# Attention with a later landing time and an earlier last step of the feature map in its scheduler

## The chip, the cores and the metric

The kernel runs on one core of one Trainium2 chip. The metric is the device time of one execution in microseconds (us). A core has five engines that run their own instruction lists in order: PE (matrix products), DVE (VectorE), ACT (ScalarE), POOL (GpSimd) and SP (SyncE), which here only issues transfers between HBM and the on-chip memory. An engine that waits for something holds up all that stands behind it in its list.

## The reference

Three stages run one after the other: attention, a mixture of experts, and a dense block of two layers. Only the first is touched by the change, and only its scores and its feature map matter here.

```python
B, H, S, D = (4, 8, 576, 64)
scores = scale * np.matmul(q, k.transpose(0, 1, 3, 2))
scores = np.where(causal, -1000000000.0, scores)
scores = scores - scores.max(-1, keepdims=True)
a = np.exp(scores)
a /= a.sum(-1, keepdims=True) + 1e-09
local = np.matmul(a, v)

def phi(x):
    return np.where(x > 0, x, np.exp(x) - 1.0) + 1.0
q_p = phi(q)
mem_ret = np.einsum('bhsd,bhde->bhse', q_p, M_prev)
mem_norm = np.einsum('bhsd,bhd->bhs', q_p, z_prev)[..., None] + 1e-06
mem_out = mem_ret / mem_norm
return (g * mem_out + (1 - g) * local).astype(np.float32)
```

The output of attention goes through `_moe_ref` (gate, one of eight experts per token) and `_moe2_ref` (two dense products), whose code the change leaves alone.

## The kernel before

**Tiles.** Attention works on eight groups, n = 0 to 7: batch n // 2, and heads 0 to 3 or 4 to 7 of it. The 576 rows of a group are cut into three row blocks, x = 0, 1, 2: rows 0 to 255, 256 to 511, 512 to 575. For each row block q and k are loaded into `qn` and `kn` (tile a in the profile), v into one of two tiles `vn`. Groups share the one `qn` and the one `kn`; so a row block of the next group's q can only be loaded when the present group has read it for the last time.

**What is done with q.** For each row block the ACT copies q into an array of rounded values (L594), POOL makes the rest (L599), and the feature map is made in three steps: `exp` on ACT (L629) into `ph`, `relu` on ACT (L631) in place in `qn`, and the last step on DVE (L634), which reads both. That last step is also the last reader of the row block of `qn`. It releases the next group's q load of the same block. k is copied by DVE (L592).

**What a slot is.** Each group has eight slots (four heads, two halves of the rows). In a slot PE makes the scores (L728), DVE takes the row maxima from them (L735, L747, L752), PE turns the maxima with q (L759), ACT evicts that (L764), PE makes the scores once more with the maxima in them (L779, L781, L786, L790), ACT takes `exp` of them (L795, tile pT), and PE multiplies with v (L817, L820). Between the slots stand the transposes of the next group's k and q (PE L644, L647; evicted by ACT L665, L666, L672).

**What else runs there.** 32 pieces of the weights of the third stage are converted beside attention: a load of 512 KB (L321), two ACT steps (L326, L329), two DVE steps (L332, L335), a POOL step (L338) and a store of 256 KB (L341).

**What sets the order.** Every step is a task of `Sched`: an engine, a duration, the tasks it depends on, and a key. `Sched.order` plays the tasks through in a model of time. A free engine takes, of its ready tasks, the one with the lowest key; a task that ends makes its users ready after a latency, `LAT` of its engine (2,300 ns for SP) or its own `lat`. The sequence that comes out is the order in which the instructions of PE, ACT, DVE and POOL are written. SP's transfers are put in place by the tool that builds the program, from the same sequence. On the chip nothing of the model's time is left, only the order. The keys of the feature map are `G[n] - L * f`, with f = `PE1`, `PE2`, `PE3` for its three steps; G[n] is the group's start in the model and L = 4 * (1320.114 + 3696.75) = 20,067 ns. The keys of group 0 are made in another way: `T0 + 5000 + 1000 * x - 1000 * f`.

Of the kernel before, what the change touches and what calls it, by code (L numbers as in the profile page):

```python
# [25 lines left out]
PVB = 2  # L26
LDT = (1310, 1310, 650)
X0, XH, PH0, FIN, RT1, RT2, RW = 86.4, 9571.6, -315.2, -443.3, 4930.3, 5386.7, 1.74
PKH, PKL, PQH, PQL, PE1, PE2, PE3 = 0.19, 1.07, 0.92, 0.72, 0.38, 0.26, -0.09
EK, WS = 39944.504, 485.0  # L30
PT0, PTX, PTH, PT2 = 0.3, -0.1, -0.17, -1427.4
MAN = {ET.PE, ET.Activation, ET.DVE, ET.Pool}
# [2 lines left out]
SP = [[[(0, 0, 0, 128), (1, 128, 0, 256)]], [[(2, 0, 0, 384)], [(3, 0, 0, 512)], [(4, 0, 0, 256)], [(4, 0, 256, 320)]]]  # L35
# [28 lines left out]
class Sched:  # L64
# [5 lines left out]
    def add(self, eng, dur, fn, deps=(), key=0.0, take=(), give=(), lat=None):  # L70
        self.tasks.append((eng, dur, fn, set(d for d in deps if d is not None), key, take, give, lat))
        return len(self.tasks) - 1
# [59 lines left out]
class K:  # L132
# [401 lines left out]
    def group(self, n, b, g, get, put):  # L534
        nc, add, st = self.nc, self.sc.add, self.st
        L, G = 4 * (TA + TB), self.G
        par, h0 = n % 2, G4 * g
        kn, qn, ph, kx, qa = self.kn, self.qn, self.ph, self.kx, self.qa
        qb, vn = self.qb[par], self.vn[par]
# [9 lines left out]
        def load(dst, src, i0, i1):  # L549
            def f():  # L550
                if i1 - i0 == 2:
                    for i in range(i0, i1):
                        nc.sync.dma_start(dst[:, i, :, 0:D], src[b, h0:h0 + G4, rng(i), :].rearrange("h p d -> p h d"))
                else:
                    nc.sync.dma_start(dst[:64, 4, :, 0:D], src[b, h0:h0 + G4, 512:576, :].rearrange("h p d -> p h d"))
            return f
        gs = G[n] - (LD * L if n else 1e6)
        for x, (i0, i1) in enumerate(W):
            lk = add("SP", LDT[x], load(kn, self.k, i0, i1), get(("kuse", n - 1, x)), gs if n else gs + 2 * x)
            lq = add("SP", LDT[x], load(qn, self.q, i0, i1), get(("quse", n - 1, x)), gs + 1 if n else gs + 2 * x + 1)  # L560
            put(("lk", n, x), lk)
            put(("lq", n, x), lq)
            if n == 0:
                self.first |= {lk, lq}
        for x, (i0, i1) in enumerate(W):
            lv = add("SP", LDT[x], load(vn, self.v, i0, i1), get(("vuse", n - 2)) + (get("set") if n == 1 else []), gs + 2 if n else gs + 6 + x)
            put(("lv", n), lv)
            if n == 0:
                self.first.add(lv)
# [703 lines left out]
    def put(self, o, xg, ix, w3, after):  # L1273
        v = [self.axpy(o, xg, ix[:, 1:2].bitcast(F32)), self.axpy(o, xg, w3, slice(64, 128))]
        info = mybir.DependencyInfo(mybir.DependencyClass.NoSync, mybir.DependencyReason.DATA)
        for i in v:
            self.tc.add_manual_dep(i.ins, after.name, info, reason="issue order")
# [423 lines left out]
```

## Time and profile before

| | |
|---|---|
| median of 3 runs | 873.3 us (871.55 to 881.11) |
| profiled execution | 869.84 us, of which its span is 868.2 us |
| attention | about 0 to 300 us of the span |
| experts | about 300 to 470 us |
| dense block | 470 us to the end |

Times in the rows below are us from the start of the span. A row of the timeline reads: start, duration, engine, line, operation, tile written from tiles read, form, number of like instructions merged into the row; in brackets the idle time of the engine ahead of it and who ended that. A row of the stretches reads: stretch and its length, then busy time and number of instructions of PE, PEld (weight loads), DVE, ACT and POOL, then the granted clock of TensorE as a share of full speed, the busy share of the DMA engines, and GB/s.

### The profile page before, as it was taken

To read this page: it belongs to the slowest core of one execution; us is meant where nothing else is said; L and a number is where in the kernel's file an instruction comes from. 1 tells how busy PE (TensorE), PEld (TensorE's weight loads), DVE (VectorE), ACT (ScalarE), POOL (GpSimd) and SP (SyncE) were. 2 spreads that over 40 slices of the span, in tenths; PEclk is the share of its full clock that TensorE was granted. 3 is DMA by queue.
4 is the path that set the end of the run, shared out by engine and by line. 5 is a ranking of instruction groups with operands and counts; after the bars stand their busy time and mean duration, and the time that the engine had idled before them with its cause. 6 is when DMAs were issued, how large, how long until landed. Compare 5 with 4: busy or idle time off the path is not lost. (4 is left out here: it accounts for less than half of the span.)

```text
span 868.2 us, 19498 instructions
## 1 busy us (share of the span) xinstructions
PE 829.6 (96%) x7368; PEld 739.0 (85%) x7368; DVE 614.3 (71%) x1739; ACT 481.3 (55%) x937; POOL 195.7 (23%) x262
## 2 busy tenths in 40 slices
PE   6999999997999799999989999999999999999997
PEld 5788877886888677667657999999999999999997
DVE  6877987787778983786774599665656565656565
ACT  8898977886865742776654455333333333333332
POOL 6546445644532613322220000000000000000000
PEclk9999999998999999999999999999999999999999
DMA  6857547765356586797744201010101010101000
GB/s 144 220 147 229 151 157 177 204 221 128 102 158 256 191 329 186 283 359 252 258 180 137 80 1 51 1 50 1 49 2 49 2 49 2 49 2 49 1 26 25
DMA packets 103946, 107.61 MB, mean 124 GB/s; under 512 B 69661, under 2 KB 69789, under 8 KB 103828
## 3 DMA queue, kind: packets, MB, share of 16 engines
q1 hardware_dynamic: 101190, 100.90, 37.0%
q0 software_dynamic: 2640, 5.21, 1.9%
q8 instruction: 67, 1.10, 0.5%
q14 instruction: 49, 0.40, 0.2%
HBM read 81.57 MB, written 25.86 MB: 124 GB/s over the span
## 5 line engine op out<-in xcount | busy, mean ns | idle before, releaser
L1616 PE MATMUL g<-sw,ah 128*128 128x256 f32 x448 | 126.0, 281 | 0.0
L1615 PE MATMUL g<-sw,ah 128*128 128x256 f32 x448 | 125.7, 281 | 0.0
L1567 DVE SCALAR_TENSOR_TENSOR ua<-ua 128x512 f32<-128x512 f32 x72 | 49.7, 690 | 80.2 <-ACT ua L1516 80.2
L1516 ACT ACTIVATE ah<-ua 128x384 fp32r<-128x384 f32 (+1 forms) x72 | 38.8, 539 | 110.4 <-PE g L1617 82.6
L1516 ACT ACTIVATE ua<-t 128x512 f32<-128x512 f32 x72 | 43.0, 597 | 101.1 <-PE t L1560 101.1
L735 DVE CUSTOM_DVE_ANT_0 v<-t,v 128x512 f32<-128x512 f32 (+4 forms) x160 | 75.3, 471 | 28.1 <-PE t L728 23.2
L1617 PE MATMUL g<-sw,al 128*128 128x256 f32 x320 | 89.8, 281 | 0.0
L1615 PEld LDWEIGHTS g<-sw,ah 128*128 128x128 f32 x448 | 84.4, 188 | 0.0
L1616 PEld LDWEIGHTS g<-sw,ah 128*128 128x128 f32 x448 | 84.3, 188 | 0.0
L795 ACT ACTIVATE pT<-t 128x384 f32<-128x384 f32 (+2 forms) x128 | 62.5, 503 | 23.9 <-PE t L786 13.1
L1557 PE MATMUL t<-x,v 128*128 128x256 f32 x288 | 71.9, 283 | 0.7 <-ACT x L1436 0.7
L1558 PE MATMUL t<-x,a 128*128 128x256 f32 x288 | 71.0, 280 | 0.5 <-DVE a L1103 0.5
L1558 PE MATMUL t<-x,v 128*128 128x256 f32 x288 | 71.1, 279 | 0.0
L1557 PE MATMUL t<-x,a 128*128 128x256 f32 x288 | 71.0, 280 | 0.0
L820 PE MATMUL pv<-vn,pT 128*64 128x65 f32 x1280 | 61.4, 232 | 0.6 <-issue 0.6
L1617 PEld LDWEIGHTS g<-sw,al 128*128 128x128 f32 x320 | 60.9, 190 | 0.0
L820 PEld LDWEIGHTS pv<-vn,pT 128*64 128x64 f32 x1280 | 46.9, 139 | 15.6 <-issue 11.0
L1557 PEld LDWEIGHTS t<-x,v 128*128 128x128 f32 x288 | 54.3, 188 | 1.2 <-ACT x L1436 0.9
L338 POOL TENSOR_TENSOR cg<-cg,v 128x512 int32<-128x512 int32 x32 | 42.5, 1330 | 56.2 <-issue 29.1
L1558 PEld LDWEIGHTS t<-x,a 128*128 128x128 f32 x288 | 54.1, 188 | 0.7 <-DVE a L1103 0.7
L1558 PEld LDWEIGHTS t<-x,v 128*128 128x128 f32 x288 | 54.1, 188 | 0.3
L1557 PEld LDWEIGHTS t<-x,a 128*128 128x128 f32 x288 | 54.1, 188 | 0.0
(371 smaller groups left out, 2317.8 us busy)
## 6 DMA issues: line engine op xcount, KB each, us to landing
c<-in_moe_w_dram SPq DMA_DIRECT2D x32, 512.0 KB, 6.5
va<-in_moe_w_dram SPq DMA_DIRECT2D x21, 512.0 KB, 7.9
v<-in_moe_w_in_dram SPq DMA_DIRECT2D x16, 512.0 KB, 4.9
v<-in_moe_w_out_dram SPq DMA_DIRECT2D x16, 512.0 KB, 4.6
xe<-x SPq DMA_DIRECT2D x18, 256.0 KB, 3.1
out_dram<-xe SPq DMA_DIRECT2D x18, 256.0 KB, 2.2
a<-in_k_dram SPq DMA_DIRECT2D x32, 128.0 KB, 4.4
a<-in_q_dram SPq DMA_DIRECT2D x32, 128.0 KB, 3.2
```

What stands on the lines that cost most here:

```text
L338: nc.gpsimd.tensor_tensor(u["g"], u["g"], u["s"], op=ALU.add)
L735: nc.vector.tensor_tensor_reduce(out=self.y[:R, 0:w], in0=s[:R, o:o + w], in1=self.mb[:R, max(0, MB[i] + c0):max(0, MB[i] + c0) + w], scal ...
L795: nc.scalar.activation(u["pT"][:, o1:o1 + w], u.pop(("t", p))[:, 0:w], AF.Exp, scale=0.125)
L820: nc.tensor.matmul(t[m:m + 64, o:o + 65], u["pT"][:, c + m:c + m + 64], vn[:, j, h], start=(j == 0), stop=(j == i))
L1516: tt_, cp = V.tensor_tensor, lambda o, i: A.activation(o, i, AF.Copy)
L1557: nc.tensor.matmul(o, wih[k][:, fs], xh[:, k], start=(k == 0), stop=False)
L1558: nc.tensor.matmul(o, wil[k][:, fs], xh[:, k], start=False, stop=False)
L1567: V.scalar_tensor_tensor(u, u, 0.01, u, op0=ALU.mult, op1=ALU.max)
L1615: nc.tensor.matmul(o, ah, wh, start=(p == z == 0), stop=False, skip_group_check=True)
L1616: nc.tensor.matmul(o, ah, wl, start=False, stop=False, skip_group_check=True)
L1617: nc.tensor.matmul(o, al, wh, start=False, stop=(p == 7), skip_group_check=True)
```

## The change

Two numbers of the scheduler's model change. Loads of k, q and v get `lat=3500` in place of SP's 2,300 ns, so in the model their users become ready 1,200 ns later. `PE3` goes from -0.09 to 0.1, so the key of the feature map's last step (DVE L634) falls by 0.19 * L = 3,813 ns in groups 1 to 7, and by 190 ns in group 0. Neither adds or removes an instruction. What comes of it is another order.

```diff
-PKH, PKL, PQH, PQL, PE1, PE2, PE3 = 0.19, 1.07, 0.92, 0.72, 0.38, 0.26, -0.09
+PKH, PKL, PQH, PQL, PE1, PE2, PE3 = 0.19, 1.07, 0.92, 0.72, 0.38, 0.26, 0.1
...
-            lk = add("SP", LDT[x], load(kn, self.k, i0, i1), get(("kuse", n - 1, x)), gs if n else gs + 2 * x)
-            lq = add("SP", LDT[x], load(qn, self.q, i0, i1), get(("quse", n - 1, x)), gs + 1 if n else gs + 2 * x + 1)
+            lk = add("SP", LDT[x], load(kn, self.k, i0, i1), get(("kuse", n - 1, x)), gs if n else gs + 2 * x, lat=3500)
+            lq = add("SP", LDT[x], load(qn, self.q, i0, i1), get(("quse", n - 1, x)), gs + 1 if n else gs + 2 * x + 1, lat=3500)
...
-            lv = add("SP", LDT[x], load(vn, self.v, i0, i1), get(("vuse", n - 2)) + (get("set") if n == 1 else []), gs + 2 if n else gs + 6 + x)
+            lv = add("SP", LDT[x], load(vn, self.v, i0, i1), get(("vuse", n - 2)) + (get("set") if n == 1 else []), gs + 2 if n else gs + 6 + x, lat=3500)
```

The order moves on every engine from group 0 to the start of group 5 and is nearly the same from there on. Three places follow.

DVE in group 5, about 202 us into the span of before. L735 is the row maxima of head 1's slot of rows 256 to 575 (its second row reads out the result), L747 and L752 finish them, L332 and L335 belong to the conversion, and L634 is the last step of the feature map of group 6, row block 2. Before:

```order
L735 ISA v_85,m_98<-t,v_85 64x256
L735 ISA m_98 64x1
L332 SCALAR_TENSOR_TENSOR v_85<-v_85 128x512
L735 ISA v_85,m_98<-t,v_85,m_98 64x320
L735 ISA m_98 64x1
L335 TENSOR_SCALAR cg<-cg 128x512
L747 TENSOR_REDUCE m_98<-m_98 128x3
L752 TENSOR_REDUCE v_84<-m_98 128x3x2
L634 SCALAR_TENSOR_TENSOR a_82<-a_82 128x256
```

After the change DVE has there:

```order
L735 ISA v_85,m_96<-t,v_85 64x256
L735 ISA m_96 64x1
L634 SCALAR_TENSOR_TENSOR a_82<-a_82 128x256
L735 ISA v_85,m_96<-t,v_85,m_96 64x320
L735 ISA m_96 64x1
L332 SCALAR_TENSOR_TENSOR v_85<-v_85 128x512
L747 TENSOR_REDUCE m_96<-m_96 128x3
L752 TENSOR_REDUCE v_84<-m_96 128x3x2
L335 TENSOR_SCALAR cg<-cg 128x512
```

The last step stands ahead of a conversion step and of the last part of the row maxima, where it stood behind both; L335 now stands behind the maxima's end.

SP at the same place, as a piece of the difference: the five loads of v of group 6, then the load of q of group 7, row block 2 (L555 into a), and the conversion's stores (L341) and loads (L321).

```order
 L553 DMA vn_90<-in_v_dram 128x4x64 x4
 L555 DMA vn_90<-in_v_dram 64x4x64
-L341 DMA wout<-cg 128x512
-L321 DMA v_85<-in_moe_w_out_dram 128x1024
-L555 DMA a_82<-in_q_dram 64x4x64
+L555 DMA a_82<-in_q_dram 64x4x64
+L341 DMA wout<-cg 128x512
+L321 DMA v_85<-in_moe_w_out_dram 128x1024
 L341 DMA wout<-cg 128x512
 L321 DMA v_85<-in_moe_w_out_dram 128x1024
```

The load of q stands ahead of one store and one load of the conversion.

ACT in group 3, about 137 to 143 us into the span of before: evictions of slots (L764), `exp` of slots (L795) and the copies of q of group 5 (L594, two to a row block). Before:

```order
L764 ACTIVATE q_2446<-t 66x256
L795 ACTIVATE pT<-t 128x320
L764 ACTIVATE q_2461<-t 66x256
L594 ACTIVATE v_84<-a_82 128x8x64 x2
L795 ACTIVATE pT<-t 128x384 x2
L326 ACTIVATE cg<-v_85 128x512
L329 ACTIVATE v_85<-v_85 128x512
L665 ACTIVATE b_86<-t 128x2x256
```

After the change ACT has there:

```order
L764 ACTIVATE q_2453<-t 66x256
L795 ACTIVATE pT<-t 128x320
L672 ACTIVATE b_86<-t 128x2x256
L795 ACTIVATE pT<-t 128x384
L329 ACTIVATE v_85<-v_85 128x512
L594 ACTIVATE v_84<-a_82 128x8x64
L795 ACTIVATE pT<-t 128x384
L594 ACTIVATE v_84<-a_82 128x8x64
L594 ACTIVATE v_84<-a_82 128x4x64
```

The first of the two `exp` stands ahead of the copies of q, with two other steps, and the second between them.

## Rows read from the trace of the kernel before

**Rows 1.** The page's first line: the span.
```profile
span 868.2 us, 19498 instructions
```

**Rows 2.** Stretches: most of attention, the stretch round 210 us, the experts.
```profile
10.00:200.00 190.00, 182.86 (x2161) 154.85 (x2159) 154.95 (x598) 163.47 (x376) 98.31 (x127) 1.00 0.67 183
200.00:220.00 20.00, 15.03 (x140) 12.77 (x138) 12.91 (x45) 11.20 (x28) 9.04 (x10) 0.83 0.48 116
...
300.00:470.00 170.00, 158.46 (x822) 115.09 (x823) 115.38 (x190) 95.10 (x141) 41.21 (x35) 1.00 0.71 250
```

**Rows 3.** Timeline of PE from 198 to 218 us.
```profile
198.20 0.69 PE L820 MATMUL pv<-vn,pT 128*64 128x65 f32 x16
...
205.38 0.35 PE L759 MATMUL t<-idr,v 128*66 128x128 f32 x3 [0.30 <-DVE v L752]
...
214.25 0.69 PE L728 MATMUL t<-c 128*128 128x384 f32 x1 [3.46 <-ACT pT L795]
...
216.50 1.14 PE L820 MATMUL pv<-vn,pT 128*64 128x65 f32 x16
```

**Rows 4.** Timeline of ACT from 207 to 214 us.
```profile
207.29 0.60 ACT L795 ACTIVATE pT<-t 128x512 f32<-128x512 f32 x1 [0.29 <-PE t L786]
213.41 0.42 ACT L594 ACTIVATE v<-a 128x256 fp32r<-128x256 f32 x1 [5.52 <-DMA a<-in_q_dram]
```

**Rows 5.** Timeline of SP from 201 to 207 us.
```profile
201.72 0.65 SPq L555 DMA_DIRECT2D vn<-in_v_dram  x1
203.63 0.34 SPq L341 DMA_DIRECT2D wout<-cg  x1
204.06 0.38 SPq L321 DMA_DIRECT2D v<-in_moe_w_out_dram  x1
206.75 0.65 SPq L555 DMA_DIRECT2D a<-in_q_dram  x1
```

**Rows 6.** Timeline of DVE and POOL from 202 to 207 us.
```profile
202.29 1.86 DVE L332 SCALAR_TENSOR_TENSOR v<-v 128x512 int32<-128x512 int32 x1
202.31 1.29 POOL L338 TENSOR_TENSOR cg<-cg,v 128x512 int32<-128x512 int32 x1
...
204.55 0.41 DVE L335 TENSOR_SCALAR cg<-cg 128x512 int32<-128x512 int32 x1
...
205.06 0.17 DVE L752 TENSOR_REDUCE v<-m 128x6 fp32r<-128x12 f32 x1
205.11 1.31 POOL L338 TENSOR_TENSOR cg<-cg,v 128x512 int32<-128x512 int32 x1
205.15 1.57 DVE L634 SCALAR_TENSOR_TENSOR a<-a 128x256 f32<-128x256 f32 x1
```

**Rows 7.** Line L634, the last step: durations, and what its engine waited for.
```profile
L634 DVE SCALAR_TENSOR_TENSOR a<-a x24: 364/684/1572, 12.8 to 236.9; 128x512 f32<-128x512 f32 x16, 128x256 f32<-128x256 f32 x8
...
  ACT a L631: 0.3, 1
```

**Rows 8.** Line L555, the loads of row block 2: issue to landing.
```profile
DMA to landing us min/median/max: 2.3/3.1/6.0
```

**Rows 9.** One stretch: the matmuls behind the wait of PE at 214 us.
```profile
214.20:218.90 4.70, 4.64 (x30) 4.09 (x31) 2.31 (x9) 3.71 (x10) 0.00 (x0) 0.50 0.00 1
```

**Rows 10.** Timeline of ACT and PE from 141 to 146 us.
```profile
141.01 1.16 ACT L594 ACTIVATE v<-a 128x512 fp32r<-128x512 f32 x2 [2.31 <-DMA a<-in_q_dram]
142.07 0.85 ACT L795 ACTIVATE pT<-t 128x384 f32<-128x384 f32 x2
142.59 0.38 PE L759 MATMUL t<-idr,v 128*66 128x128 f32 x3 [0.58 <-ACT pT L795]
...
145.07 0.49 PE L728 MATMUL t<-c 128*128 128x512 f32 x1 [0.81 <-ACT b L672]
```

**Rows 11.** Line L631, the relu on ACT ahead of the last step: durations.
```profile
L631 ACT ACTIVATE a<-a x24: 406/618/689, 8.4 to 235.4; 128x512 f32<-128x512 f32 x16, 128x256 f32<-128x256 f32 x8
```

**Rows 12.** Timeline of PE in the experts, its longest wait there.
```profile
387.56 5.17 PE L1150 MATMUL s<-a,xs 128*128 128x512 f32 x21 [1.91 <-ACT b L1099]
```

## The prediction

> **What bounds the kernel now.** I read the stretches first, since the change can only act in attention, the first 300 us. Between 10 and 200 us PE is busy for 182.86 of 190 us [rows 2]: PE sets the pace, and no more than 7.14 us of idle time stand there, in short pieces. The stretch from 200 to 220 us is the exception: PE is busy for 15.03 of 20 us, and the granted clock falls to 0.83 in the mean. So I followed that one hole back, engine by engine, in the timelines.
>
> PE stands still for 3.46 us before 214.25, and waits there for ACT's `exp` [rows 3]. ACT had finished the `exp` before that at 207.89 and then stood still for 5.52 us, until 213.41, because the next instruction in its list, the copy of q of group 7, row block 2, waited for the landing of that q [rows 4]. The load of this q was issued at 206.75, although SP had been done with the v loads ahead of it at 202.37 and with the conversion's transfers at 204.44 [rows 5]. It could not go earlier, because the buffer was still being read: DVE's last step of the feature map of group 6, row block 2, ran from 205.15 to 206.72 [rows 6]. So the chain is: last step late on DVE, load late, ACT's copy late, `exp` behind the copy late, PE idle. It has a second price. Behind the hole the granted clock is 0.50, which is the 1.2 GHz level, for the whole stretch from 214.20 to 218.90, with PE busy for 4.64 us in it [rows 9]. Sixteen like matmuls take 1.14 us there and 0.69 us at 198.20 at the full 2.4 GHz level [rows 3].
>
> **The change part by part.** No instruction is added or removed, so each term is a wait that goes or comes.
>
> *The late load.* On DVE the last step of group 6, row block 2, now stands directly behind the row maxima that ended just ahead of 202.29. Ahead of it go one L332, one L735, one L335 and the end of the maxima, which was over at 205.23 [rows 6]. The step so starts at about 202.3 in place of 205.15. Its duration is bounded by 0.36 us (the shortest of the 24) and 1.57 us (the longest, which is this very one) [rows 7]. It ends between 202.7 and 203.9. SP has nothing ahead of the load but the v loads, over at 202.37, so the load is issued between 202.7 and 203.9, which is 2.9 to 4.1 us earlier. From issue to landing, loads of this size take 2.3 to 6.0 us with a median of 3.1 [rows 8]; in before this one took about 6.6 us (206.75 to the copy's start at 213.41), with a store and a 512 KB load issued shortly ahead of it [rows 4, 5], both of which now stand behind it. With the median the q lands between 205.8 and 207.0, before ACT gets there at 207.89. In the worst corner, 203.9 and 6.0, it lands at 209.9 and ACT still waits 2.0 us. I take the median, as the two transfers ahead are gone: the wait goes. What is late next is PE's own list. This gives 3.46 us of idle time, and the clock: 4.64 us of matmuls at the low level shorten by the share (1.14 - 0.69) / 1.14 = 0.39, which is 1.8 us. Together **-5.3 us**; with the worst corner a stand of up to 2.0 us stays, so the bounds are -5.3 and -3.3.
>
> *What the moved step delays.* The last step now stands ahead of the end of the row maxima, for which PE waits (0.30 us of idle time at 205.38 [rows 3]). Out of the DVE work ahead of that end goes L335 with 0.41 us, and in comes the last step with 0.36 to 1.57 us. So the maxima end 0.05 us earlier to 1.16 us later. Both long durations in the rows, 1.86 and 1.57 us, ran beside a POOL step of 1.3 us [rows 6]; one POOL step, at 202.31, will still be there, and it can lengthen the last step or L332, not both. I take the lower half: **+0.3 us**.
>
> A rule of the Trainium skill speaks against this placing. "SBUF — State Buffer", section "SBUF: two separate sides", says that a VectorE instruction with two inputs in SBUF and a GpSimd instruction that reads SBUF exclude each other: the one that starts first keeps the shared ports until it ends. The trace agrees so far as the 1.57 us go. By that rule the last step, if it starts behind POOL's 202.31, runs only after 203.60, and ends at about 203.96; the load would go out at the late end of the bounds above, and the term for the maxima would be +1.2 in place of +0.3, the sum so 0.9 us worse.
>
> *The wait at 141 us.* ACT waits 2.31 us for q of group 5, row block 1, and behind that copy stand two `exp`, for the first of which PE waits (0.58 us); a further 0.81 us is lost at 145.07 to an eviction that ACT reaches late [rows 10]. After the change the first `exp` stands ahead of the copies, so PE's wait no longer hangs on the load, and ACT has more to do before it needs the q. I take both: **-1.4 us**, with 0 as the other bound.
>
> *The rest of groups 1 to 5.* Here every engine's list is shuffled. Of the 7.14 us that PE idles between 10 and 200 us [rows 2], 1.39 are counted above. The 5.75 us left can go, and as many can come. Two things are visible in the order. Consumers of q mostly move back behind two or three `exp`, which takes waits for landings away. Against that, the relu of group 2 (L631) moves back behind about a dozen ACT steps, and with it the last steps and the q loads of group 3, so that the slack ahead of ACT's first copy in group 3 becomes small. No row prices the net; I take **+1.5 us**, some two waits of the size of those in rows 10, and keep -5.75 and +5.75 for the range.
>
> *The setting of group 0 and the v loads* I cost at nothing: v is used only by the last products of a slot, long after it is issued, and group 0's keys move by 190 ns.
>
> Sum: -5.3 + 0.3 - 1.4 + 1.5 = -4.9 us. On the profiled execution of 869.84 us (span 868.2 [rows 1] and 1.64 us around it) that is 864.9 us; the median of the runs shown lies 3.5 us higher, at 873.3, and I carry the difference over: **868.4 us**, 0.6% less.
>
> **The rivals.**
>
> *Given back later (about 873 us).* The hole at 210 us closes, but the experts do not start sooner in effect, because their weights set the pace: DMA engines are busy for 0.71 of 300 to 470 us, and PE's longest wait there, 1.91 us at 387.56, is for ACT's rounding of weights [rows 2, 12]. For it: attention's end and the stream of weights overlap. Against it: PE is busy for 158.46 of the 170 us, so the weights are rarely what is late; and their loads go out when engines release buffers, so they move forward with the rest. Time: 872 to 874.
>
> *Slower (877 us or more): DVE blocked by ACT.* The last step needs the relu on ACT. Pushed forward in DVE's list, it may come to the head before its relu is done, and then holds up the row maxima behind it, for which PE waits. In before that happened once, for 0.3 us [rows 7]. There are 21 last steps in groups 1 to 7. A relu lasts 0.62 us in the median [rows 11], so a step that comes one ACT instruction too early loses about that. The gain of 6.7 us is used up at 6.7 / 21 = 0.32 us on average that reaches PE; at 0.5 us it is 10.5 us, and the time 873.3 - 6.7 + 10.5 = 877. For it: in group 2 the relus move back strongly. Against it: in the model the step is only taken when its relu is done, and 0.3 us in 24 steps shows that the model's margin held so far.
>
> *The load stays late (871 us).* The last step lasts 1.57 us again, since a POOL step starts beside it at 202.31 as one did at 205.11 [rows 6], and the load takes 6.0 us [rows 8]: 2.0 us of ACT's wait stay, PE's gain at the hole is 3.3 in place of 5.3 us, and the maxima are 1.2 us late: -3.3 + 1.2 - 1.4 + 1.5 = -2.0, or 871.3. For it stand both long durations beside POOL, against it the two transfers that no longer stand ahead. The port rule of the Trainium skill, cited above, would make the first half of it certain.
>
> *More than that (863 us).* The shuffled groups lose most of their idle time as well: -5.3 + 0.3 - 1.4 - 4 is -10.4.
>
> **How the numbers follow.** Forecast 0.55, given back 0.18, slower 0.13, load stays late 0.07, more 0.07. The likeliest is the forecast: 868.4, its own range 865 to 872. Left out should be 0.2: the range from 863 to 877 cuts off part of the slower case and of the last one. A change of 1%, 8.7 us, is about what a measurement of this kernel can tell from none. Faster by over 1% (below 864.6) is the last case and the forecast's edge: 0.12. Slower by over 1% (above 882) is half of the slower case: 0.07. Within 1%: 0.81.
>
> **What would show it.** In the profile of the changed kernel: the load of q of group 7, row block 2, issued right behind the v loads and about 3 us sooner in the course of group 5; ACT's 5.52 us wait for it gone or below 2 us; no stretch of granted clock 0.50 between 200 and 230 us; PE idle there below 2 us; the wait for q in group 3 gone. The experts and the dense block should take as long as before. The prediction is wrong if new waits for last steps (DVE for L631) or for q of group 3 add up to more than 3 us, if another hole of PE above 2 us with its stretch of low clock appears in groups 1 to 5, or if attention ends 5 us sooner and the whole does not.

## The result, and the profile after

| | before | after |
|---|---|---|
| median | 873.4 us (871.55 to 881.11, 6 runs) | 865.5 us (862.98 to 867.26, 6 runs) |
| profiled execution | 869.84 us, span 868.2 | 864.59 us, span 863.0 |

The ratio is 0.9886, with a 95% interval of 0.9855 to 0.9917. Ratios here, and counts and means of executions below, leave disturbed executions out, so that they can differ a little from what the medians give. The forecast was 868.4 us, with a range of 863 to 877 us. The profiled execution was forecast at 864.9 us and took 864.59; the median fell by 7.9 us where 4.9 were forecast.

The page's first line after, the span, answers to [rows 1]:

```profile
span 863.0 us, 19512 instructions
```

The stretches after (columns as in [rows 2]); the last two are new:

```profile
10.00:200.00 190.00, 184.65 (x2178) 156.76 (x2176) 156.37 (x605) 166.34 (x380) 99.29 (x131) 1.00 0.69 185
200.00:220.00 20.00, 18.54 (x232) 16.14 (x232) 17.05 (x64) 16.43 (x38) 13.98 (x16) 1.00 0.45 90
300.00:470.00 170.00, 158.32 (x789) 115.78 (x780) 112.03 (x174) 91.74 (x135) 37.54 (x32) 0.99 0.68 238
292.80:296.20 3.40, 3.17 (x25) 2.61 (x26) 3.26 (x13) 2.02 (x3) 1.31 (x3) 0.50 1.01 396
381.60:385.00 3.40, 3.40 (x9) 2.64 (x8) 3.37 (x5) 1.06 (x2) 0.97 (x1) 0.50 1.00 339
```

Between 200 and 220 us PE is busy for 18.54 in place of 15.03 us, at a granted clock of 1.00 in place of 0.83. The hole is closed. But two stretches of 0.50, the 1.2 GHz level, stand in the experts now, where the profiled execution before had none.

How the hole closed is seen in four timelines of the changed kernel. DVE, about 199 us:

```profile
199.38 1.59 DVE L634 SCALAR_TENSOR_TENSOR a<-a 128x256 f32<-128x256 f32 x1
...
201.36 0.69 DVE L332 SCALAR_TENSOR_TENSOR v<-v 128x512 int32<-128x512 int32 x1
...
202.15 0.17 DVE L752 TENSOR_REDUCE v<-m 128x6 fp32r<-128x12 f32 x1
```

POOL beside it:

```profile
199.40 1.29 POOL L338 TENSOR_TENSOR cg<-cg,v 128x512 int32<-128x512 int32 x1
```

SP, which issues the load of q of group 7, row block 2, as soon as the last step is over, ahead of the conversion's transfers:

```profile
201.03 0.64 SPq L555 DMA_DIRECT2D a<-in_q_dram  x1
201.77 0.57 SPq L341 DMA_DIRECT2D wout<-cg  x1
```

ACT, where the copy of that q waits 0.78 us in place of 5.52 [rows 4]:

```profile
205.75 0.42 ACT L594 ACTIVATE v<-a 128x256 fp32r<-128x256 f32 x1 [0.78 <-DMA a<-in_q_dram]
```

PE, whose longest waits there are these; in [rows 3] one was 3.46 us:

```profile
202.46 0.34 PE L759 MATMUL t<-idr,v 128*66 128x128 f32 x3 [0.29 <-DVE v L752]
...
206.60 0.32 PE L759 MATMUL t<-idr,v 128*66 128x128 f32 x2 [0.62 <-ACT pT L795]
...
213.75 0.50 PE L728 MATMUL t<-c 128*128 128x512 f32 x1 [0.55 <-ACT b L672]
```

Where the time came from can be followed by the ends of the row maxima (L752) of one and the same slot in both traces. The end for group 5, head 1, second half moves from 205.1 to 202.1 us, so groups 1 to 5 gave about 2.9 us. The next end but two moves from 219.0 to 210.8: the hole gave another 5.3. Attention's end stays 8.1 to 8.2 us sooner (last row maxima 294.6 to 286.5, first L1119 301.1 to 293.0). Then 2.9 us are given back. 1.3 us go between the first and the last L523 of the experts (323.3 and 334.0 before, 315.4 and 327.4 after), where PE has a new wait of 1.02 us for ACT's L499. 1.4 us go between the first and the last L1150 (372.3 and 459.4 before, 365.6 and 454.1 after), where the second stretch of low clock above stands. Both stretches stand behind waits of PE that the kernel before has too (2.27 us at 301.14, and [rows 12]), without low clock in its profiled execution:

```profile
293.03 1.94 PE L1119 MATMUL t<-idr,xe 128*128 128x128 f32 x8 [2.22 <-DMA xe<-xs,ixe]
...
380.82 5.55 PE L1150 MATMUL s<-a,xs 128*128 128x512 f32 x16 [1.92 <-ACT b L1099]
```

### The profile page after: what moved, and what is told of

The parts are those of the page before. It is cut to its first block, busy times and chain, and to the rows that moved or that the text cites. A ratio compares the mean times of both kernels' runs of the same rounds, so it can differ in the third digit from the quotient of the medians.

```text
span 863.0 us, 19512 instructions
## 1 busy us (share of the span) xinstructions
PE 829.5 (96%) x7368; PEld 739.8 (86%) x7368; DVE 612.4 (71%) x1739; ACT 482.4 (56%) x937; POOL 193.4 (22%) x262
## 5 line engine op out<-in xcount | busy, mean ns | idle before, releaser
L735 DVE CUSTOM_DVE_ANT_0 v<-t,v 128x512 f32<-128x512 f32 (+4 forms) x160 | 75.5, 472 | 28.4 <-PE t L728 22.8
L795 ACT ACTIVATE pT<-t 128x384 f32<-128x384 f32 (+2 forms) x128 | 62.5, 503 | 23.8 <-PE t L786 12.8
L338 POOL TENSOR_TENSOR cg<-cg,v 128x512 int32<-128x512 int32 x32 | 42.5, 1329 | 65.3 <-issue 38.8
```

The source lines that it names most:

```text
L338: nc.gpsimd.tensor_tensor(u["g"], u["g"], u["s"], op=ALU.add)
L735: nc.vector.tensor_tensor_reduce(out=self.y[:R, 0:w], in0=s[:R, o:o + w], in1=self.mb[:R, max(0, MB[i] + c0):max(0, MB[i] + c0) + w], scal ...
L795: nc.scalar.activation(u["pT"][:, o1:o1 + w], u.pop(("t", p))[:, 0:w], AF.Exp, scale=0.125)
```

## The experiments

All kernels compute all of the reference. In the first group two instructions are put by hand where the other kernel has them, or one half of the change is made alone. `moved` takes a task out of the finished order and puts it behind another.

**m_step: the hole alone, from before.** 1423 is the last step of group 6, row block 2, 1605 the load of q of group 7, row block 2.

```diff
-            order = self.sc.order()
+            order = moved(self.sc.order(), (1423, 1254), (1605, 1394))
```

> The kernel before, with two instructions moved by hand: the last step of group 6, row block 2, stands ahead of L332 on DVE, and the load of q of group 7, row block 2, right behind the v loads on SP. Nothing else moves. Theory (the late load makes the hole): the stand of PE of 3.46 us behind the exp at 214 us and the stretch of granted clock 0.50 behind it go, the experts' first matmul (L1119, at 301.1 us in the profile of before) starts at about 295.8, and the time is 5.3 us lower, 868 against 873.4. Rival (the hole only moves: PE's own list, or ACT, is late next): the first L1119 comes after 299 and the time is less than 2 us lower. Rival (given back in the experts): L1119 at 296, the end not before 866 in the span.

Measured: 870.2 us against 878.2, ratio 0.9933 (0.9902 to 0.9964). In the trace the hole is gone. Stretches of this kernel, the second of them new:

```profile
200.00:220.00 20.00, 18.48 (x226) 15.65 (x220) 17.80 (x60) 16.82 (x39) 12.57 (x16) 1.00 0.47 123
297.40:304.20 6.80, 4.64 (x37) 3.77 (x37) 1.50 (x4) 2.31 (x4) 1.17 (x3) 0.50 1.03 400
```

Attention's row maxima end 5.0 us sooner behind the hole, as expected. In this one execution that was given back: the first L1119 came 4.4 us sooner and the first L1206 0.1 us later, with low clock from 297.4 us and two waits of PE at the experts' first transposes of 2.84 and 2.22 us, in place of 2.27 and 1.05. The median of 12 executions kept it. One profile of each kernel alone would have misled here.

**m_back: the changed kernel without the hole's two moves.**

```diff
+            order = moved(self.sc.order(), (1423, 1257), (1605, 2010))
```

> The changed kernel, with the same two instructions moved back to where they stood in the kernel before: the last step of group 6, row block 2, behind the end of the row maxima, the load of q of group 7, row block 2, behind a store and a load of the conversion. All the rest of the change stays. Theory: the hole of some 3.5 us and its stretch of low clock are there again about 3 us earlier in the course (near 210 us), L1119 starts at about 298.2, and the time is about 2.9 us under the kernel before, 870.5. Rival (the rest of the change closes the hole too, since ACT's list is another): no stand of PE above 2 us between 200 and 220, L1119 near 293 as in the changed kernel, time about 865.5.

Measured: 870.0 us against 878.2, ratio 0.9912 (0.9879 to 0.9945). The hole is back, with its low clock. A wait on PE's timeline and a stretch:

```profile
211.99 0.69 PE L728 MATMUL t<-c 128*128 128x384 f32 x1 [3.70 <-ACT pT L795]
```

```profile
209.60:216.30 6.70, 4.31 (x29) 3.75 (x29) 2.01 (x7) 4.50 (x11) 0.39 (x1) 0.50 0.35 61
```

So in the changed kernel it is these two instructions that close the hole. They do it in two ways: here the load was issued 2.7 us later (at 203.73 us), and it took 7.4 us from its issue to the copy's start in place of 4.7. Behind the store and the load of the conversion it took 6.7 and 7.4 us (before, m_back), ahead of them 4.7 and 4.9 (after, m_step). But what is left of the change without them is worth 0.9%, some 8 us, not the 2.9 that I had read from the profile. Here the expectation was off.

**e_pe3 and e_lat: the halves.**

```diff
 # e_pe3, from before.py
+... PE3 = ..., 0.1
 # e_lat, from after.py
+... PE3 = ..., -0.09
```

> One half of the change: PE3 0.1 with the old landing time. The order is that of before up to about group 5. Theory: this half closes the hole and is worth all of the 5.3 us: L1119 first at about 296, time 868. Rival (the two halves are only good together): some wait for the feature map's relu or for a q load appears in groups 5 to 7 and takes 2 us or more of it, time 870 or more.

> The other half: landing time 3,500 ns for k, q and v with the old PE3. Up to group 5 the order is nearly that of the changed kernel, and the last step of group 6, row block 2, stands late as in before. Theory: groups 1 to 5 are 2.9 us shorter, as in the profile of the changed kernel, and the hole near 210 us stays: L1119 first at about 298, time 870.5. Rival (the gain of groups 1 to 5 comes from the earlier last steps there, PE3): L1119 at 300 to 302, time 872 to 874.

Measured: PE3 alone 877.4 us against 878.2, ratio 0.999 (0.9964 to 1.0015): nothing. The landing time alone 865.5 us against 878.2, ratio 0.9874 (0.9842 to 0.9906): as much as the whole change. Both theories of mine fell. In the trace of the landing time alone the last step is as late as in before (1.58 us from 202.13), and so is the load on SP:

```profile
200.62 0.34 SPq L341 DMA_DIRECT2D wout<-cg  x1
201.05 0.38 SPq L321 DMA_DIRECT2D v<-in_moe_w_out_dram  x1
203.74 0.65 SPq L555 DMA_DIRECT2D a<-in_q_dram  x1
```

Yet the hole is closed, because ACT's copy of that q stands behind eleven more ACT instructions and finds the q landed:

```profile
210.64 0.49 ACT L795 ACTIVATE pT<-t 128x384 f32<-128x384 f32 x1
211.02 0.71 ACT L594 ACTIVATE v<-a 128x256 fp32r<-128x256 f32 x2
```

With PE3 alone the copy still waits 1.88 us at 216.73 and PE behind it 1.57 us at 217.99: the hole is smaller, but not closed.

**m_copy: the later copy alone, from before.** 1631 is the first copy (L594) of q of group 7, row block 2.

```diff
+            order = moved(self.sc.order(), (1631, 1632))
```

> The kernel before, with one ACT instruction moved by hand: the first copy of q of group 7, row block 2, stands behind the other copy of that row block, some ten ACT instructions later. The last step on DVE and the load stay as late as in before. The run with the landing time alone closed the hole with the load still late, so there are two theories. Theory A (it is the copy's place in ACT's list that makes the hole; the earlier load is one cure and the later copy another): the stand of PE at 214 us and its stretch of low clock go, the end of attention comes about 5 us sooner, and the time is some 6 us under the kernel before, as with the step and the load moved. Theory B, of the prediction (only the earlier load helps; something else behind the load, the rest that POOL makes of q or PE's transposes, is late next): PE stands still for 2 us or more between 212 and 222, and the time is within 3 us of before.

Measured: 878.2 us against 880.6, ratio 0.9961 (0.992 to 1.0002). In the trace PE's wait is gone although the load is issued at 215.27, behind the conversion's transfers: PE's longest wait between 212 and 222 us is 0.80 us, and the row maxima behind it come 4.0 us sooner relative to those ahead. Theory A holds for the wait. It does not hold for the clock, since 3.4 us at a granted clock of 0.51 still stand there (219.4 to 222.8), nor for the time: the median hardly moved, and the interval of the ratio reaches 1. The trace shows where this one execution lost more than was won. A wait and a stretch of this kernel:

```profile
113.48 0.80 PE L925 MATMUL t<-idr,xb 128*128 128x128 f32 x3 [1.10 <-DVE m L735]
```

```profile
113.70:127.30 13.60, 13.60 (x100) 10.51 (x98) 6.30 (x36) 4.35 (x11) 4.80 (x7) 0.50 0.49 162
```

The same stretch of the kernel before, which up to here has the same order and the same wait of 1.10 us at 111.75:

```profile
113.70:127.30 13.60, 13.58 (x188) 11.22 (x188) 10.59 (x57) 9.96 (x24) 4.18 (x8) 1.00 0.36 121
```

PE is busy all the time in both, but does 100 matmuls in place of 188, and the slots behind come 5.6 us later. That the wait brings the low clock is not shown by this: the same wait has none behind it in before.

**after_again, before_again and k_warm: the low clock.** k_warm is the changed kernel with 16 more transposes at two places: in the first `x_tr` (warm is 16 there and 0 elsewhere), and in the same way ahead of the L1150 of one expert.

```diff
-    def x_tr(self, xg):
-        t = self.T_tile()
+    def x_tr(self, xg, warm=0):
+        t = kept(self, self.T_tile(), warm)
...
+def kept(self, t, n):
+    for _ in range(n):
+        self.nc.tensor.transpose(t[:, 0:128], self.idf, self.idf)
+    return t
```

> The changed kernel once more, beside the runs of this call, for the time that it has at low clock: over the six runs so far the granted clock was 0.995 in the mean, and 0.988 over 23 of before. Theory (a part of the gain is low clock that waits of PE bring in some executions and not in others): the mean clock is again above 0.993, the spans lie between 861 and 868, and what varies between executions goes with the clock. Rival (the clock differs by chance between chips): a mean clock near 0.988 and spans up to 875.

> The kernel before, looked at once more. Its profiled execution was the shortest of its runs (868.2 us span, granted clock 0.996, one stretch of 0.50), and 23 others had a median span of 876.6 and a mean clock of 0.988. Theory: in an ordinary execution further stretches of 0.50 stand behind waits of PE of a microsecond or more that are the same in both executions, above all the wait of 1.10 us at 111.75 us for the row maxima, which the changed kernel does not have, and those at 142 and 388. Rival: the longer executions lose their time elsewhere, in waits for transfers, at full clock.

> The changed kernel with 32 more transposes on PE whose results are overwritten: 16 ahead of the experts' first transposes (where PE waits 2.22 us at 293 us) and 16 ahead of the products that wait 1.92 us for ACT's rounding at 381 us. Sixteen take about 2.0 us, so they fit into the waits. Theory (the two stretches of 0.50 behind these waits come from PE's standing still): both are gone, the granted clock is 0.997 or more, and the time is up to 3 us under the changed kernel, about 862.5. Rival (the clock falls for another reason): the stretches stay or come elsewhere, and the time is that of the changed kernel or up to 1 us more.

Measured: the changed kernel again 866.5 us against 880.6, ratio 0.9829 (0.9775 to 0.9883), mean granted clock 0.994. The kernel before took 875.5 us in its one more execution, with two stretches of low clock in attention, of which only the second stands behind the hole:

```profile
26.80:40.40 13.60, 13.60 (x89) 11.17 (x87) 7.26 (x23) 10.51 (x24) 6.86 (x9) 0.50 0.72 203
214.50:221.30 6.80, 3.40 (x25) 2.84 (x25) 1.68 (x6) 4.25 (x11) 0.82 (x2) 0.50 0.42 77
```

The places that I had named for it (112, 142, 388 us) were not those of this execution, and the longest wait of PE in the 14 us ahead of 26.8 was 0.56 us (at 15.1 us); what brings that one I can't say.

k_warm: 864.9 us against 880.6, ratio 0.9823 (0.9771 to 0.9876); mean clock 0.997, and the six executions lie between 864.1 and 866.0, where the changed kernel's lay between 863.1 and 868.6. PE at the first of the two places (the transposes at the other stood in a branch that the data did not take):

```profile
289.39 1.97 PE L1708 MATMUL t<-idr 128*128 128x128 f32 x16
291.86 0.66 PE L1119 MATMUL t<-idr,xe 128*128 128x128 f32 x4 [0.51 <-DMA xe<-xs,ixe]
294.74 0.63 PE L1119 MATMUL t<-idr,xe 128*128 128x128 f32 x4 [2.22 <-DMA xe<-xs,ixe]
```

The first wait was filled; the second tile's wait of 2.22 us was not, and a stretch of 0.50 stands behind it. The stretch at 381 us is absent in this execution, though nothing was put ahead of it. So the theory is not shown: the higher mean clock and the narrower spread fit it, but no single stretch was taken away by filling its wait. The medians of k_warm and of the changed kernel can't be told apart, which is what the rival said of the time.

**m_335 and m_all: can the gain of groups 1 to 5 be had at single places?** 1938 is a conversion step (L335) ahead of the row maxima at 109 us; 1159 and 1160 are the copies of q of group 5, row block 1.

```diff
 # m_335, before.py
+            order = moved(self.sc.order(), (1938, 655))
 # m_all, before.py
+            order = moved(self.sc.order(), (1423, 1254), (1605, 1394), (1938, 655), (1159, 831), (1160, 1159))
```

> The kernel before, with one DVE instruction moved by hand: the conversion's L335 that ran 2.21 us from 109.15 us, ahead of the row maxima for which PE waits 1.10 us at 111.75 us, now stands behind these maxima. Five executions of an order that is that of before up to here have been looked at: two (the one with the later copy and the one with PE3 alone) have a stretch of granted clock 0.50 of 13.65 us behind this wait and lose 5.6 us in it, three have none. Theory (the wait costs itself and, in some executions, the stretch): the wait goes, no stretch of 0.50 stands near 113 us, full-clock time falls by 1.1 us and the median by about 3 us. Rival (the stretch comes without the wait, or the wait moves one place on): a stretch near 113 us or a wait of about 1 us behind it, and the time of before within 1 us.

> The kernel before, with five instructions moved by hand: the two of the hole (last step and load of q), the L335 at 109 us, and the two copies of q of group 5, row block 1, behind the two exp at 142 us. All other instructions stand as in before. Theory (the change's gain is these places: the hole 5.1 us, the waits at 112 and 142 us 1.1 and 1.4 us, and the low clock that the first two bring): attention ends some 7 to 8 us sooner than in the profile of before, the mean clock is above 0.993, and the time is within 2 us of the changed kernel's, about 1.4% under before. Rival (the gain is spread over the shuffled order of groups 1 to 5 and can't be had from these places): the ratio to before stays at 0.993, as with the two of the hole alone.

Measured: m_335 879.6 us against 878.2, ratio 1.0049 (1.0016 to 1.0081), a little slower. No stretch of low clock stands near 113 us in its trace, and the row maxima there come only 0.35 us sooner relative to those ahead. The wait had moved one place on, as the rival said: the next conversion step took 1.90 us in place of 0.68 (110.95, L332), and PE waits at the following instruction:

```profile
114.21 0.35 PE L759 MATMUL t<-idr,v 128*66 128x128 f32 x3 [0.92 <-DVE rl L864]
```

m_all: 870.6 us, ratio 0.9917 (0.9889 to 0.9944); with the two instructions of the hole alone it was 0.9933. The copies behind both `exp` took the wait of 0.58 us away, but the eviction behind them came hardly sooner (0.3 us, measured from the row maxima ahead), and PE now waits there:

```profile
145.94 0.50 PE L728 MATMUL t<-c 128*128 128x512 f32 x1 [1.48 <-ACT b L672]
```

1.48 us stand in place of 0.58 and 0.81, and 0.92 us, at 114.53, in place of the 1.10. As the rival said, these moves do not bring the gain of groups 1 to 5. But they moved PE's waits on and did not remove them, so what the waits are worth was not measured. ACT's waits for q (L594) are nearly gone in this kernel all the same, 1.3 us in all of attention where before has 8.7:

```profile
  DMA a<-in_q_dram: 1.3, 2
```

**e_lat5 and e_pe3b: larger doses of both numbers.**

```diff
 # e_lat5, from after.py: the three loads
+... lat=5000
 # e_pe3b, from after.py
+... PE3 = ..., 0.3
```

> The changed kernel with a landing time of 5,000 ns in place of 3,500. Theory (the later landing helps because ACT reaches the copies of q after they have landed, and 3,500 already does that: ACT's copies wait 1.0 us in all there): nothing more is to be gained, the time is that of the changed kernel within 2 us, either way as the order falls. Rival (more distance to the landing gives more): no wait of ACT for q at all and 2 us or more less.

> The changed kernel with PE3 0.3 in place of 0.1, a larger dose of the half that gave nothing alone. Rival of the prediction (a last step pushed further forward on DVE comes to the head of its list before ACT's relu, L631, is done, and blocks the row maxima): DVE's waits for L631 add up to more than 2 us, where they are 0 to 0.3 us in all the kernels so far, and the time is 3 us or more above the changed kernel, near 870. Theory (the step is taken when its relu is done and there is margin on the chip): waits for L631 below 0.5 us, and a time that differs from the changed kernel only by how the rest of the order falls, 864 to 869.

Measured: e_lat5 869.0 us against 878.2, ratio 0.9902 (0.9866 to 0.9937), e_pe3b 867.4 us against 881.8, ratio 0.9855 (0.979 to 0.9919). With 5,000 ns ACT's copies wait for no q at all any more, but POOL, which makes the rest of q from the copy, waits 8.4 us in all for it (0.6 in the changed kernel), and nothing is won over 3,500: the theory's first half holds. The median lies some 3 us above the changed kernel's, more than the 2 allowed for; but the two did not run beside each other, and the intervals of their ratios overlap, so that a loss is not shown. Nor is POOL's wait shown to cost time: PE's longest new wait in attention is one of 3.18 us at 17.56 us (0.57 in the changed kernel, at 15.13), and the profile names no releaser for it. With PE3 0.3 DVE waits for no L631 at all: the rival of a blocked DVE has no wait to show even at this dose. Its trace has a wait of PE of 2.21 us at 151.97 us for row maxima instead, with low clock behind it.

## Why the prediction was right, and which of its steps were not

**The late load: right in size and in mechanism, but not the only cure.** The term was -5.3 us; the traces show -5.3 between the same two slots in the changed kernel and -5.2 in m_step, and m_back brings the hole back. The step started at 199.38, which is 202.3 less the 2.9 us of the groups ahead, and lasted 1.59 us, the upper bound; the load took 4.7 us from 201.03 to the copy's start, not the median of 3.1, and 0.78 us of ACT's wait stayed. PE waited 0.62 us for it. What I missed is that the hole had a second cure. I had looked for the one that the order of the changed kernel showed, which PE3 brings, and took the landing time for a shuffle with an unknown sign. Alone the landing time closes the hole by putting the copy later, and alone it is worth the whole change; PE3 alone is worth nothing that 12 executions show.

**What the moved step delays: +0.3 forecast, about 0 measured.** PE's wait for these maxima is 0.29 us (0.30 before). The step took its 1.59 us, but L332, which had 1.86 us beside POOL in [rows 6], now takes 0.69: the long duration changed hands, as the prediction allowed, and the 0.41 us of L335 went out. The rule of the Trainium skill that was cited ("SBUF — State Buffer", section "SBUF: two separate sides") says that two such instructions of DVE and POOL exclude each other. The traces agree so far as these go: the last step ended 0.30, 0.28 and 0.29 us after POOL's L338 in before, after and m_step, and took 1.57 to 1.59 us each time; in m_back, with no L338 beside it, it took 0.42. Which of the two started first they do not settle: in after and m_step the last step's start is recorded 0.01 to 0.02 us ahead of POOL's. The price of 0.9 us drawn from it did not come, since L332 got back 1.17 us.

**The wait at 141 us: -1.4 forecast, about -1.0 measured, and not from the copies alone.** Both waits of PE are gone after the change, and the row maxima around them (133 to 149.5 us) gain 1.0 us. In m_all moving the copies gave about 0.4 us there, as PE then waited for the eviction L672. The changed order has an eviction of that line ahead of the copies as well.

**The rest of groups 1 to 5: +1.5 forecast, -1.9 us in the profile; this step failed, in its sign.** I priced the net of a shuffle at two waits of the kind seen, by no row. Beside the waits at 141 us, the largest that went is one of 1.10 us for row maxima, which no term had. The wait before, and the stretch round it before and after:

```profile
111.75 1.48 PE L925 MATMUL t<-idr,xb 128*128 128x128 f32 x12 [1.10 <-DVE m L735]
```

```profile
100.00:115.00 15.00, 13.69 (x181) 11.27 (x179) 13.65 (x48) 12.26 (x28) 9.73 (x13) 1.00 0.72 200
```

```profile
100.00:115.00 15.00, 15.00 (x208) 12.87 (x210) 11.91 (x47) 12.65 (x28) 9.92 (x14) 1.00 0.79 226
```

Another of 0.59 us (65.59, for `exp`) went too, and one of 0.62 us for row maxima came (124.32 after). What the later landing time does directly is seen in ACT's waits for q (L594) in all of attention, before and after:

```profile
  DMA a<-in_q_dram: 8.7, 4
```

```profile
  DMA a<-in_q_dram: 1.0, 2
```

But these waits are not the gain of groups 1 to 5. Of the 8.7 us, 5.52 are the hole and 2.31 the copy at 141 us, which have their own terms; two short waits with 0.85 us in all are left for the rest. And m_all, with 1.3 us of them, gained hardly more than the hole alone (0.9917 against 0.9933), while m_back, with 5.0, has 0.9912. Which of the moved instructions bring the gain stays open. The prediction saw in the order that consumers of q stand back, and set a hypothetical loss in group 3 against it that did not come: after the first of these waits, at 5.65 us, ACT has none until 205.75 in the changed kernel.

**Carrying the 3.5 us between profile and median over: this step failed too, and it is why the median came 2.9 us under the forecast.** It took the difference for a constant. It differs from one execution to the next, and goes with the low clock. The profiled execution of before had a span of 868.2 us; of 67 others with a span on record the shortest had 870.5, and their mean is 876.7 at a mean clock of 0.987. The changed kernel has 864.1 at 0.994 in 12. At a like clock, 0.994 or more, the means are 872.1 (5 executions of before) and 862.9 (7 after), m_step 868.0 (8) and m_back 866.2 (2). So some 9 us of the 12.6 are there at a like clock, and some 3 come with less of the low clock; with 5 executions, and from several chips (the means of before lie between 875.8 and 879.6 us in the four comparisons), this is a rough split. The hole is one source of low clock: all four profiled executions that have it (before, before_again, m_back, m_335) show 0.50 behind it, and after, m_step, e_lat and m_all do not there. The wait of 1.10 us at 111.75 us may be another, but that is argued: of the five profiled executions of an order that has it, two had 13.6 us at 0.50 behind it. The changed kernel has no such wait.

Here the forecast also had luck. The 12.6 us are two and a half times the 4.9 that were forecast, and the changed kernel's second comparison gave a ratio of 0.9829. That the first table shows 7.9 us, nearer to the forecast, is due to its executions of before: their median is 873.4 us, where the later comparisons have 878.2 to 881.8.

**The rivals.** Given back later: it happened in part, 2.9 us in the profiled execution, although the experts were to take as long as before; but not by the weights' stream as I had it: a new wait for L499 stands at the place of 1.3 us of it, and low clock behind a wait that both kernels have at that of 1.4. DVE blocked by ACT: the last step waits for no L631 above 0.3 us in any kernel. (The price of this rival took a gain of 6.7 us where the sum had 4.9.) The load stays late: the 1.59 us came, the rest did not. The -3.4 us by which the groups beat their term and the +2.9 of the experts nearly cancelled in the profiled execution; that 864.9 met 864.59 is chance.

**Open.** PE3 alone gains about 3.6 us of attention behind group 5 in its profiled execution (against before, the row maxima of second halves are 7.9 us late ahead of the hole and 4.3 at the end of attention), and its 12 executions show nothing of it. What takes it back was not found. Nor was it tried which of the many moved instructions of groups 1 to 4 carry the gain of m_back, or why m_335 is 0.5% slower.

## What to carry to other kernels

Where a model sets the order of in-order engines, look for the consumer that stands at the head of a list waiting for a transfer, and for both cures: an earlier issue, and a later place of the consumer. Here a latency of 3,500 ns in the model, where the loads of row block 2 land in 3.1 us in the median [rows 8], bought the second at many places at once; 5,000 ns took ACT's last waits away too and bought nothing more. And before a profile is turned into a forecast of a median, see how that execution stands in the spread of spans and granted clocks: here it was the shortest of 68.

## What was not expected of the hardware

The same wait of PE is followed by low clock in one execution and not in the next. The 1.10 us at the L925 of the order before were followed by 13.6 us at 0.50 in two of five profiled executions. A stretch of the same length stood at 26.8 us in before_again, with no wait above 0.56 us in the 14 us ahead of it. At the experts' first transposes PE waited 2.27 and 1.05 us in the profile of before, with no low clock, and 2.22 us in that of after, with 3.4 us at 0.50. A second profiled execution of the changed kernel has waits of 2.50 and 1.83 us there, and this stretch:

```profile
293.80:304.00 10.20, 8.79 (x67) 6.45 (x69) 5.35 (x16) 2.39 (x5) 2.77 (x6) 0.50 1.04 402
```

The kernel before has spans from 870.5 to 885.7 us in the 67 executions, with a mean of 872.1 at a granted clock of 0.994 and more (5) and 878.4 at 0.989 and less (45). The changed kernel, with fewer and shorter waits in attention, has spans from 861.4 to 867.0 in 12. That it is the waits of a microsecond or two that bring the low clock, and so cost more in the mean than their own length, fits this, but no run here shows it.
